# Softmax denominators of two head groups at once on 64 by 32 array tiles, with copied rows and a reordered first batch

## The chip, the cores and the metric

One core of one Trainium2 chip. The metric is the device time of one execution in microseconds (us), the median of several executions. All runs told here are of the state that the records call fast. PE is TensorE, PEld its weight loads, DVE VectorE, ACT ScalarE, POOL GpSimd, SP SyncE. A "q" behind a name (ACTq, SPq) is that engine's queue of transfers.

## The reference

Attention with normalised q and k, followed by a feed-forward block, in float32:

```python
# q, k, v: (batch 8, heads 12, seq 448, head_dim 64)
q_n, k_n = rmsnorm(q, g_q), rmsnorm(k, g_k)
scores = q_n @ k_n.T / 8
attn = exp(scores - max); attn = attn / (sum(attn) + 1e-9)
x = (attn @ v) reshaped to (3584 tokens, 768)
h = x @ w_in                          # w_in: (768, 2048)
g = max(h, 0) + alpha * min(h, 0)
out = g @ w_out                       # w_out: (2048, 768)
```

## The kernel before

Work is cut into 24 groups of four heads, three groups to a batch element. For each group the kernel squares and reduces q and k, takes the inverse root on ScalarE, scales (on GpSimd, early on partly on VectorE), transposes (from group 8 on by a transposing DMA on SyncE's queue), and then makes seven score tiles. ScalarE takes each tile's exponential. TensorE sums them over the keys (dn, the denominators) and multiplies them with v (av). ScalarE inverts dn as exp(-ln(dn)), and VectorE multiplies av with it.

```python
def root(y, nms="qk"):                       # ScalarE, 0.33 + 0.23 us
    ...
    nc.scalar.activation(out=rr, in_=ss, func=AF.Ln, scale=1.0 / D, bias=epsb[:, 0:1])
    nc.scalar.activation(out=rr, in_=rr, func=AF.Exp, scale=-0.5)

def scale(y, nm):
    t = ld.tile([128, J, 2, D], FP16, name="qs", tag="qs", bufs=4)
    eng = nc.vector if (y, nm) in ((0, "k"), (1, "q")) else nc.gpsimd
    eng.tensor_mul(out=..., in0=nat[y, nm], in1=rr_t[y][...])

def score(y, j):                             # two buffers in all
    sc = pss.tile([128, 2, 512], FP32, name="sc", tag="sc")
    ...                                      # four matmuls, 64 by 64 tiles

def over_keys(name, y, weights):             # 28 matmuls, four at once
    acc = psa.tile([128, 2, 512], FP32, name=name, tag="acc")   # one buffer
    e = expT[y]
    for j in range(J):
        for g in range(2):
            for par in range(2):
                nc.tensor.matmul(out=acc[ds(64 * par, 64), g, :S],
                    lhsT=weights(g, par, j), rhs=e[ds(64 * g, 64), j, par, :],
                    start=(j == 0), stop=(j == J - 1))
    return acc

def den(y):
    rden[y] = over_keys("dn", y, lambda g, par, j: ones[ds(64 * g, 64), :])
def log(y):
    r = att.tile([128, 2, S], FP32, name="rden", tag="rden")
    nc.scalar.activation(out=r, in_=rden[y][:, :, :S], func=AF.Ln)
    rden[y] = r
def invert(y):
    nc.scalar.activation(out=rden[y], in_=rden[y], func=AF.Exp, scale=-1.0)
def attv(y):
    av = over_keys("av", y, ...v...)
    nc.vector.tensor_mul(out=xT[b][:, :, i, :], in0=av[:, :, :S], in1=rden[y])
```

The order is written by hand as a list of bursts. Each burst has two or three score tiles, at most one dn or one av, the root of a later group, and some feed-forward units that fill TensorE while ScalarE works: "up" (hT, six matmuls, then ah on ScalarE and gT on VectorE) and "down" (op, 16 matmuls):

```python
for n in range(NB):
    ...
    for t in tiles[:2]:
        score(*t); soft(*t)                  # soft: the exponential
    if n in dens: den(dens[n])
    if n in avs:  attv(avs[n])
    for t in tiles[2:]:
        score(*t); soft(*t)                  # the third tile
    if n in dens: log(dens[n]); invert(...)
    if n in roots: root(y); scale(y, "q"); scale(y, "k"); turn_dma(y)
    ...                                      # feed-forward units
```

## Time and profile before

| | before |
|---|---|
| time, median of three runs | 456.1 us (455.84 to 456.34) |
| span of the profiled run, mean granted clock | 454.8 us, 0.994 |
| TensorE busy, ScalarE busy | 94%, 64% |

The span is cut into 40 equal slices in this part of the page. A digit is the busy share in tenths. PEclk is the granted TensorE clock in tenths of full speed.

```profile
PE   7677889989999999999999999999999999999996
...
PEclk9989999999999999999999999999999999999999
```

TensorE is nearly full from the eighth slice on, at full clock. What little the score matmuls wait is told by their group (busy us, mean ns, then the idle time before them and who ended it):

```profile
L217 PE MATMUL sc<-qT,kT 64*64 64x448 f16 x672 | 53.8, 364 | 8.6 <-ACT expT L229 5.9
```

To see more than the page tells, I also summed the trace's times from each matmul's start to the next one's start, and split each into **work** (at most a matmul's normal pace), **mode switches** (0.09 us where the tiling changes), **waits**, and **half clock** (the excess of matmuls that run close together while the granted clock is halved). This bookkeeping is mine, from the trace's records and not from a view. Counted a second time with other limits for "close together", waits and half clock move against each other by up to some 5 us; the sums stay. For the kernel before it gives 404.4 of work, 11.3 of switches, 31.2 of waits and 1.6 us of half clock, 448.6 in all. The rest of the span lies ahead of the first matmul and behind the last.

### The profile page before, as it was taken

The page shows a single profiled execution, that of the slowest core. Times are in us where ns is not written, and L with a number is a line of the kernel's source. Part 1 is how long each engine was busy: PE and PEld are TensorE (multiplying, and loading weights), DVE is VectorE, ACT ScalarE, POOL GpSimd, SP SyncE. Part 2 cuts the span into 40 slices and gives each one's busy share as a digit, 9 for nine tenths or more (in the row PEclk, how much of TensorE's full clock was granted, in tenths as well). Part 3 has the DMA queues.
Part 4 walks back from the last instruction along what each step waited for, and adds up shares of the span by engine and source line. Part 5 has one row for each costly group of instructions (what it writes and reads, how often), then busy time and mean ns, then how long its engine had stood idle before and what let it go on. Part 6 is the DMA issues. An engine that isn't in the chain of part 4 may idle for free.

```text
span 454.8 us, 9094 instructions
## 1 busy us (share of the span) xinstructions
PE 426.9 (94%) x3843; PEld 229.8 (51%) x3843; DVE 206.0 (45%) x295; ACT 289.9 (64%) x402; POOL 171.9 (38%) x127
## 2 busy tenths in 40 slices
PE   7677889989999999999999999999999999999996
PEld 3333444555445555455545555455555555455563
DVE  3735353735374545355454545345564333343421
ACT  4878897567677757748786758658785847423300
POOL 5888764560560550750571450750541100000000
PEclk9989999999999999999999999999999999999999
DMA  8999994195547633785666633665352410111122
GB/s 190 239 251 235 220 255 101 23 188 124 132 80 165 156 64 94 87 176 148 120 115 141 157 79 80 114 158 139 76 91 46 76 37 1 37 35 36 35 71 69
DMA packets 60169, 52.77 MB, mean 116 GB/s; under 512 B 32720, under 2 KB 56672, under 8 KB 60128
## 3 DMA queue, kind: packets, MB, share of 16 engines
q1 hardware_dynamic: 47584, 39.37, 37.1%
q0 software_dynamic: 11808, 11.81, 16.5%
q10 hardware_dynamic: 736, 1.02, 1.0%
q8 instruction: 30, 0.49, 0.5%
q14 instruction: 11, 0.09, 0.1%
HBM read 45.62 MB, written 11.01 MB: 125 GB/s over the span
## 4 chain that ended last, share of the span: by engine, by line
PE 78%; ACT 12%; DMA 3%; DVE 3%; POOL 1%; issue 1%; SPq 0%; POOLq 0%
PE op L301 31%; PE hT L284 18%; PE hTa L284 9%; PE sc L217 7%; ACT expT L229 6%; PE av L240 5%; PE dn L240 5%; DMA nat<-in_k_dram 3%; ACT ah L292 2%; PE opa L301 2%; DVE gT L293 2%; ACT rden L255 1%; PE tps L193 1%; ACT rden L260 1%; POOL qs L158 1%
## 5 line engine op out<-in xcount | busy, mean ns | idle before, releaser
L229 ACT ACTIVATE expT<-sc,expb 128x896 f16<-128x896 f32 x168 | 157.9, 1007 | 21.2 <-PE sc L217 21.1
L301 PE MATMUL op<-w_out_sb,gT 128*128 128x384 f16 x848 | 145.9, 326 | 2.1 <-DVE gT L293 2.0
L158 POOL TENSOR_TENSOR qs<-nat,rr 128x896 f16<-128x896 f32 x46 | 79.0, 1738 | 178.8 <-issue 158.3
L284 PE MATMUL hT<-xT,w_in_sb 128*128 128x448 f16 x558 | 117.1, 353 | 3.6 <-DVE gT L293 3.5
L301 PEld LDWEIGHTS <-gT 128*128 128x128 f16 x896 | 84.6, 98 | 65.5 <-issue 12.3
L284 PEld LDWEIGHTS <-w_in_sb 128*128 128x128 f16 x768 | 73.7, 98 | 73.7 <-issue 9.6
L292 ACT ACTIVATE ah<-hT,cols 128x448 f16<-128x448 f32 x93 | 59.0, 636 | 59.6 <-PE hT L284 59.5
L293 DVE TENSOR_TENSOR gT<-hT,ah 128x448 f16<-128x448 f32 x93 | 58.0, 624 | 77.8 <-ACT ah L292 77.8
L135 POOL TENSOR_TENSOR sq<-nat 128x896 f32<-128x896 f32 x44 | 73.1, 1682 | 2.5 <-DMA nat<-in_q_dram 2.3
L328 DVE COPY osb<-op 128x384 f32<-128x384 f32 x51 | 28.4, 557 | 85.3 <-PE op L301 85.3
L217 PE MATMUL sc<-qT,kT 64*64 64x448 f16 x672 | 53.8, 364 | 8.6 <-ACT expT L229 5.9
L292 ACT ACTIVATE ah<-hTa,cols 128x448 f16<-128x448 f32 x35 | 22.2, 633 | 49.4 <-PE hTa L284 49.4
L141 DVE TENSOR_REDUCE ss<-sq 128x14 f32<-128x896 f32 x48 | 49.7, 1076 | 6.5 <-ACT sq L133 6.5
L284 PE MATMUL hTa<-xT,w_in_sb 128*128 128x448 f16 x210 | 45.4, 352 | 0.0
L217 PEld LDWEIGHTS <-kT 64*64 64x64 f16 x672 | 19.2, 105 | 38.4 <-issue 28.7
L268 DVE TENSOR_TENSOR xT<-av,rden 128x896 f16<-128x896 f32 x24 | 26.2, 1090 | 26.1 <-PE av L240 26.1
L240 PE MATMUL av<-expT,vt 64*64 64x448 f16 x672 | 36.0, 350 | 1.9 <-ACT rden L255 1.9
L240 PE MATMUL dn<-expT,ones 64*64 64x448 f16 x672 | 36.0, 350 | 0.2 <-DVE gT L293 0.2
L293 DVE TENSOR_TENSOR gT<-hTa,ah 128x448 f16<-128x448 f32 x35 | 21.8, 624 | 31.3 <-ACT ah L292 31.3
L240 PEld LDWEIGHTS <-vt 64*64 64x64 f16 x672 | 20.6, 107 | 13.8 <-issue 3.3
L240 PEld LDWEIGHTS <-ones 64*64 64x64 f16 x672 | 20.6, 108 | 12.1 <-issue 1.1
L255 ACT ACTIVATE rden<-dn 128x896 f32<-128x896 f32 x24 | 22.3, 931 | 2.4 <-PE dn L240 2.4
(39 smaller groups left out, 133.1 us busy)
## 6 DMA issues: line engine op xcount, KB each, us to landing
out_dram<-osb SPq DMA_DIRECT2D x54, 192.0 KB, 2.7
nat<-in_q_dram SPq DMA_DIRECT2D x46, 224.0 KB, 5.9
nat<-in_k_dram SPq DMA_DIRECT2D x46, 224.0 KB, 6.0
vt<-in_v_dram POOLq DMA_DIRECT2D x16, 336.0 KB, 7.4
w_in_sb<-in_moe_w_in_dram POOLq DMA_DIRECT2D x4, 768.0 KB, 15.0
w_out_sb<-in_moe_w_out_dram POOLq DMA_DIRECT2D x4, 768.0 KB, 10.8
nat<-in_q_dram ACTq DMA_DIRECT2D x2, 224.0 KB, 4.6
nat<-in_k_dram ACTq DMA_DIRECT2D x2, 224.0 KB, 5.8
```

Source lines behind the costliest of these rows:

```text
L135: nc.gpsimd.tensor_mul(out=sqf, in0=src, in1=src)
L141: nc.vector.tensor_reduce(out=ss_t[y][:, "qk".index(nm)].rearrange("p h j -> p (h j)").unsqueeze(2), in_=sqs[y, nm], axis=AXIS_X, op=ALU.add,)
L158: eng.tensor_mul(out=t.rearrange("p j h d -> p h j d"), in0=nat[y, nm], in1=rr_t[y][:, "qk".index(nm)].unsqueeze(3).broadcast_to((128, 2, ...
L217: nc.tensor.matmul(out=sc[ds(64 * g, 64), par, :S].rearrange("p (j c) -> p j c", j=J), lhsT=kT[ds(64 * par, 64), j, g, :], rhs=qT[ds(64 * ...
L229: nc.scalar.activation(out=expT[y][:, j], in_=scs[y, j][:, :, :S], func=AF.Exp, scale=QK_SCALE, bias=expb[:, 0:1],)
L240: nc.tensor.matmul(out=acc[ds(64 * par, 64), g, :S], lhsT=weights(g, par, j), rhs=e[ds(64 * g, 64), j, par, :], start=(j == 0), stop=(j == ...
L255: nc.scalar.activation(out=r, in_=rden[y][:, :, :S], func=AF.Ln)
L284: nc.tensor.matmul(out=hT[:, :S], lhsT=w_in_sb[:, c, ts(ft, 128)], rhs=x[:, c, :], start=(c == order[0]), stop=(c == order[-1]),)
L292: nc.scalar.activation(out=ah, in_=hT[:, :S], func=AF.Copy, scale=alpha_sb[:, ft : ft + 1])
L293: nc.vector.tensor_max(out=gT[:, ft, ds((b & 1) * S, S)], in0=hT[:, :S], in1=ah)
L301: nc.tensor.matmul(out=op[:, :OH], lhsT=gT[:, ft, ts(t, 128)], rhs=w_out_sb[:, ft, ds(oh * OH, OH)], start=(ft == 0), stop=(ft == NF - 1),)
L328: nc.vector.tensor_copy(out=o[:, ds(oh * OH, OH)], in_=op[:, :OH])
```

## The change

Its intent: the denominators need only 32 columns of ones per group, so two groups fit side by side on 64 by 32 tiles, eight matmuls at once, and a pair costs TensorE what one group cost. The first two batch elements (groups 0 to 5) stay single. The pair's sums then lie in 32 partitions per group and half, while the product with av wants 64; so ScalarE writes two inverses, and four DMA copies, issued on ScalarE's own queue, fill the other 32 partitions.

```diff
+    PD = min(6, NG)
+    EB = 3
-        sq = ld.tile([128, 2 * J, D], FP32, name="sq", tag="sq", bufs=4)
+        sq = ld.tile([128, 2 * J, D], FP32, name="sq", tag="sq", bufs=3)
-        eng = nc.vector if (y, nm) in ((0, "k"), (1, "q")) else nc.gpsimd
+        eng = nc.vector if (y, nm) in ((0, "k"), (1, "q"), (2, "q"), (3, "q")) else nc.gpsimd
-            expT[y] = att.tile([128, J, 2, S], FP16, name="expT", tag="expT")
+            expT[y] = att.tile([128, J, 2, S], FP16, name="expT", tag="expT", bufs=EB)
+        dn = psa.tile([128, 2, 512], FP32, name="dn2", tag="acc")
+        for j in range(J):
+            for par in range(2):
+                for n, y in enumerate(ys):
+                    for g in range(2):
+                        nc.tensor.matmul(
+                            out=dn[ds(64 * par + 32 * n, 32), g, :S],
+                            lhsT=ones[ds(64 * g, 64), :32],
+                            rhs=expT[y][ds(64 * g, 64), j, par, :], ...)
+    def invert(ys):
+        ...
+        for n, y in reversed(list(enumerate(ys))):
+            nc.scalar.activation(out=rden[y], in_=r, func=AF.Exp, scale=-1.0)
+        if len(ys) == 2:
+            for n, y in enumerate(ys):
+                for c in range(2):
+                    nc.scalar.dma_start(
+                        out=rden[y][ds(64 * c + 32 * (1 - n), 32)],
+                        in_=rden[y][ds(64 * c + 32 * n, 32)],
+                    )
-        ah = ffn.tile([128, S], FP16, name="ah", tag="ah", bufs=3)
+        ah = ffn.tile([128, S], FP16, name="ah", tag="ah", bufs=2)
-    turn_at[2] = av_at[0]
+    turn_at[2] = av_at[0] + 1
+        for y in roots.get(n, ()):           # now ahead of log and invert
+            root(y)
+            ...
         if n in dens and not lead:
             log(dens[n])
-        if n in roots:                       # was behind them
...  # cut: the list of bursts (72 in place of 66), the places of the jobs,
...  # the order of the first batch, the last output piece
```

## The prediction

> **What bounds the kernel now.** I read the page first (busy time, then the chain of waits), then the groups of instructions, then the timeline of a few bursts. A burst here is two or three score tiles, then perhaps a denominator pass (dn) or a product with v (av), then some feed-forward units: "up" (hT, 6 matmuls, 1.13 us) and "down" (op, 16 matmuls, 2.60 us).
>
> ```profile
> PE 426.9 (94%) x3843; PEld 229.8 (51%) x3843; DVE 206.0 (45%) x295; ACT 289.9 (64%) x402; POOL 171.9 (38%) x127
> ...
> PE 78%; ACT 12%; DMA 3%; DVE 3%; POOL 1%; issue 1%; SPq 0%; POOLq 0%
> ...
> L229 ACT ACTIVATE expT<-sc,expb 128x896 f16<-128x896 f32 x168 | 157.9, 1007 | 21.2 <-PE sc L217 21.1
> ...
> L240 PE MATMUL dn<-expT,ones 64*64 64x448 f16 x672 | 36.0, 350 | 0.2 <-DVE gT L293 0.2
> ...
> L255 ACT ACTIVATE rden<-dn 128x896 f32<-128x896 f32 x24 | 22.3, 931 | 2.4 <-PE dn L240 2.4
> ```
>
> TensorE holds 78% of the chain that ended last and hardly waits: dn had 0.2 us of idle time before it in the whole run. ScalarE is next at 64%. Until about 92 us the chain is mixed (ScalarE's exponentials, DMA, GpSimd); from there to the end it is almost only TensorE. So TensorE time saved after 92 us counts, as long as ScalarE keeps up within each burst. How close that is, a burst shows (start us, length us, engine, what):
>
> ```profile
> 150.42 0.57 PE L217 MATMUL sc<-qT,kT 64*64 64x448 f16 x8
> ...
> 150.83 1.49 PE L240 MATMUL dn<-expT,ones 64*64 64x448 f16 x28
> 151.06 2.80 ACT L229 ACTIVATE expT<-sc,expb 128x896 f16<-128x896 f32 x3
> ...
> 153.73 0.93 ACT L255 ACTIVATE rden<-dn 128x896 f32<-128x896 f32 x1
> 154.70 0.95 ACT L260 ACTIVATE rden<-rden 128x896 f32<-128x896 f32 x1
> ...
> 157.42 0.57 PE L217 MATMUL sc<-qT,kT 64*64 64x448 f16 x8
> ...
> 159.14 0.36 PE L217 MATMUL sc<-qT,kT 64*64 64x448 f16 x4
> ```
>
> Counted from its first score, this burst has exponentials until 3.44 us, the logarithm until 4.24, the inverse until 5.23. The next burst begins at 7.00, and its third score tile is reached at 8.72. That third tile matters: there are two score buffers, so it needs the first exponential of its own burst. Where ScalarE is late, TensorE stops exactly there, with everything behind it. The burst at 88 us, which has no feed-forward units to hide behind, shows it:
>
> ```profile
> 93.22 2.79 ACT L229 ACTIVATE expT<-sc,expb 128x896 f16<-128x896 f32 x3
> ...
> 94.26 0.38 PE L217 MATMUL sc<-qT,kT 64*64 64x448 f16 x4 [0.36 <-ACT expT L229]
> ```
>
> **What the Trainium skill says.** "TensorEngine Tiling (Array Packing)", section Tiling Modes: 64 by 32 gives eight tiles that work at once, 64 by 64 four, and a change of the mode drains the engine. The trace agrees for four: the chain has dn's 28 matmuls in 1.32 us, seven rounds of 0.189 us, with 0.189 us also the time of one matmul of 448 columns (six hT in 1.13). A change between 64 by 64 and the whole array costs 0.09 us (third score at 152.15, next op at 152.44, less 0.19). Eight at once is shown by no run yet. "Perfetto Trace Analysis", section Per-engine timelines, DMA Instruction — HWDGE: the sequencer that issues a transfer is free for its next instruction only at the end of the reported window; the data move outside it. The trace agrees: ScalarE's table load starts when its queue has finished issuing, 0.64 us each.
>
> ```profile
> 1.51 0.64 ACTq L101 DMA_DIRECT2D nat<-in_k_dram  x1
> ...
> 2.18 1.28 ACT L450 ACT_TABLE_LOAD   x1 [2.18 <-issue]
> ```
>
> "TensorE: Matmul & The Clock Gate", section The HAM clock gate: an idle window of about 3.4 us halves the clock. Here the clock was 0.61 between 30 and 34 us, after TensorE had done little from 26.9 on.
>
> **The change, part by part.**
>
> Removed: groups 6 to 23 become nine pairs. A pair has 56 matmuls, as two groups had, but if eight run at once it takes seven rounds, 1.32 us in place of 2.65. Nine times 1.32 is 11.9 us of TensorE. ScalarE saves one logarithm of 0.93 us a pair.
>
> Added on TensorE: dn now stands in another mode between second and third score, two changes of 0.09 us in eight pairs (the ninth has no scores): 1.5 us. The schedule has 72 bursts, it had 66; each is two changes: 6 x 0.19 = 1.1 us. Net 9.3 us saved.
>
> Added on ScalarE: in one burst it now does both inverses, and issues four transfers behind them. Those have to wait for its own inverses, so the sequencer stands still until then, and then spends some 0.55 us on each issue (nearly all issues from 48 to 224 KB took 0.47 to 0.67 us, whatever their size): 2.2 us. In seven of nine pairs the burst also has the root of a later group (0.33 + 0.23 us). One pair then looks like this, for a burst with one down and one up, all from rows above: exponentials until 3.44, root 4.0, logarithm 4.8, inverses 6.8, issues 9.0, ah of the up unit 9.7, first exponential of the next burst 10.6. TensorE's burst is 7.00 less one up (1.13) plus two changes: 6.06; its third score is reached 1.72 later, at 7.8. It waits 2.8 us. With one down alone both sides are earlier (6.65 and 9.7): 3.0 us. With two up units and no root (first pair): ah lies between logarithm and inverses, ScalarE comes at 10.7, TensorE at 6.3: 4.4 us.
>
> There is a second hold. The built program's waits show that each transfer on ScalarE's queue reuses one of eight semaphores, and waits for the transfer that used it before. In three pairs (8 and 9, 12 and 13, 16 and 17) the fourth copy's predecessor is the transpose of k of the group whose root stands in the same burst: root at 4.0, two GpSimd products of 1.74 us until 7.5, transpose landed 3.3 us later (median) at 10.8. ScalarE is then free at 11.3 rather than 9.0: 2.3 us more.
>
> Sum of the waits: 4.4 + 5.3 + 2.8 + 5.1 + 3.0 + 5.1 + 3.0 + 3.0, and none for the last pair, which has no scores after it: 31.7 us.
>
> The landing itself, about 2 us as for small stores, falls beside the next burst and holds only the product with av on VectorE: small.
>
> Start and end: the scaling of q for groups 2 and 3 goes from GpSimd to VectorE, beside that of k. In the chain such a scaling is a piece of 1.7 us; twice that is 3.4, I take 3 us. The last output copy is one piece in place of two on two engines: 0.5 us less.
>
> All waits as worked out: 456.1 - 9.3 - 3.5 + 31.7 = 475. No waits at all: 443. **I choose 466**, about seven tenths of the waits. They rest on a timetable that assumes nothing else shifts, and a schedule so carefully made may have been tried where they are smaller; but the third score waiting for the first exponential is in the trace already.
>
> **Rivals.** (1) *TensorE's saving goes through* and ScalarE absorbs the rest, as its 64% suggest. For it: over the five bursts of a pair ScalarE has about 23 us of work against TensorE's 30. Against: an average doesn't help, two buffers let TensorE run ahead by one tile. It gives about 443 to 447. (2) *Issues are cheap* (0.1 us for 32 rows) and no semaphore holds: each wait shrinks by 1.8 us and the three holds go, the sum becomes about 11 us: 454. Against: I found no issue under 0.47 us in the trace. (3) *Eight tiles do not run at once*, for want of instructions or read ports: TensorE saves nothing, plus 2.6 us of mode changes; waits then shrink by 1.3 us a pair: around 475 again. (4) *The longer waits throttle the clock*: four of 4.4 to 5.3 us, each followed by up to 3 us at half speed: up to 6 us on top, 481. (5) *Transfers are late* and av's product holds the one accumulator: some 1 to 2 us a pair more; against it, DMA is at a half after 100 us and small stores land in 2 to 2.7 us.
>
> **Range and chances.** No waits and a good start is the low end, 447 with a little margin given away; all waits with a throttled clock the high end, 482. Faster by over 2% needs under 447, so nearly no waits: 0.14. Within 2% is 447 to 465: half of the waits or cheap issues: 0.36. Slower: 0.50.
>
> **What would show it.** Right: 504 dn matmuls in nine stretches of 1.32 us; issues on ScalarE's queue of about 0.55 us, 36 of them; behind them idle time of ScalarE put down to issue; third scores waiting 2 to 5 us for expT, some 30 us in all where before had 5.9. Wrong: stretches of dn near 2.6 us (eight tiles), issues near 0.1 us, or third scores that don't wait. The prediction fails upward if the clock drops after those waits, downward if ScalarE's work in the pair's burst overlaps in a way that the timetable doesn't have.

## The result

| | before | after |
|---|---|---|
| time, median | 456.22 us (455.84 to 458.04, 4 runs) | 513.26 us (510.84 to 514.56, 4 runs) |
| span and mean clock, profiled run | 454.8 us, 0.994 | 509.1 us, 0.939 |

The changed kernel is slower: ratio 1.1235, 95% interval 1.1182 to 1.1289. A ratio is the mean time of one kernel's fast runs over that of the other's of the same rounds, so it is not quite the ratio of the medians quoted.

The page of the changed kernel, busy share and slices:

```profile
PE 438.9 (86%) x3837; PEld 224.1 (44%) x3837; DVE 207.8 (41%) x297; ACT 284.0 (56%) x392; POOL 169.0 (33%) x125
...
PE   7866798898697798799499699599697799999996
...
PEclk9887999898799799999699899889898999999999
```

Where TensorE stood at 9 throughout, dents come again and again from the eleventh slice on, and in the slices beside them the clock is down. TensorE's *busy* time even rose, from 426.9 to 438.9 us, though it has fewer rounds to do: matmuls at half speed are longer. The groups of instructions, scores and dn, and then the waits (in all, how often, longest):

```profile
L219 PE MATMUL sc<-qT,kT 64*64 64x448 f16 x672 | 56.2, 383 | 49.6 <-ACT expT L231 43.4
...
L263 PE MATMUL dn<-expT,ones 64*32 64x448 f16 x504 | 15.0, 375 | 0.0
```

```profile
PE sc L219 <- ACT expT L231: 43.4, 20, 6.8
```

The scores' wait for an exponential grew from 5.9 to 43.4 us. The timeline of the second pair (start us, length us; an issue's row covers all of its count, with the time between them) shows how it comes about. The view begins at 156 us and ends at 171.5, and counts only what it holds: the pair's dn has 56 matmuls, and the last row's op has 16.

```profile
155.64 1.49 PE L263 MATMUL dn<-expT,ones 64*32 64x448 f16 x49
...
159.09 0.92 ACT L275 ACTIVATE rden<-dn 128x896 f32<-128x896 f32 x1
...
160.04 1.93 ACT L283 ACTIVATE rden<-rden 128x896 f32<-128x896 f32 x2
...
162.01 5.64 ACTq L288 DMA_DIRECT2D rden<-rden  x4
...
162.41 1.23 SPq L170 DMA_TRANSPOSE kT<-qs  x1
...
167.69 2.80 ACT L231 ACTIVATE expT<-sc,expb 128x896 f16<-128x896 f32 x3 [5.72 <-DMA rden<-rden]
...
168.75 0.59 PE L219 MATMUL sc<-qT,kT 64*64 64x448 f16 x4 [6.77 <-ACT expT L231]
...
169.27 2.74 PE L332 MATMUL op<-w_out_sb,gT 128*128 128x384 f16 x8
```

The inverses end at 161.97. Then ScalarE issues four copies, and is free again only at 167.65: by the records of the single issues three took until 163.9, and the fourth began at 167.13. It waits for the semaphore of the transpose of k of a later group, which landed at 167.11. The next burst's exponentials stand behind them, so the third score starts at 168.75, after 6.77 us of an idle TensorE. The op behind it takes 2.74 us for eight matmuls; 16 took 2.60 before. The three stretches of this pair, as a table by stretch (us, then busy time and count of PE, PEld, DVE, ACT and POOL, then the clock, the DMA share and GB/s):

```profile
155.00:162.00 7.00, 6.99 (x122) 3.53 (x121) 1.34 (x3) 6.16 (x8) 4.63 (x3) 1.00 0.84 196
162.00:169.00 7.00, 0.25 (x4) 0.13 (x3) 1.09 (x1) 1.30 (x2) 2.02 (x2) 0.83 1.01 228
169.00:175.00 6.00, 6.00 (x26) 2.78 (x22) 0.86 (x2) 1.50 (x2) 0.00 (x0) 0.63 0.42 105
```

Full work, then nearly nothing, then full busy time at a clock of 0.63: that is the price of one pair. My bookkeeping, in us:

| | work | switches | waits | half clock | sum |
|---|---|---|---|---|---|
| before | 404.4 | 11.3 | 31.2 | 1.6 | 448.6 |
| after | 391.9 | 13.8 | 75.8 | 21.8 | 503.3 |
| difference | -12.5 | +2.5 | +44.6 | +20.2 | +54.7 |

The eight pairs that have scores after them waited 4.3, 6.8, 3.3, 6.4, 3.9, 6.0, 3.9 and 3.3 us, 38.0 in all. In the second, fourth and sixth, the three longest, the fourth issue was held as it is here.

### The profile page after: what moved, and what is told of

Same layout as the page of the kernel before. It is cut to its first block, busy times and chain, and to the rows that moved or that the text cites. A ratio compares the mean times of both kernels' runs of the same rounds, so it can differ in the third digit from the quotient of the medians.

```text
span 509.1 us, 9140 instructions
## 1 busy us (share of the span) xinstructions
PE 438.9 (86%) x3837; PEld 224.1 (44%) x3837; DVE 207.8 (41%) x297; ACT 284.0 (56%) x392; POOL 169.0 (33%) x125
## 5 line engine op out<-in xcount | busy, mean ns | idle before, releaser
L332 PE MATMUL op<-w_out_sb,gT 128*128 128x384 f16 x848 | 154.3, 338 | 0.0
L315 PE MATMUL hT<-xT,w_in_sb 128*128 128x448 f16 x576 | 126.1, 363 | 6.9 <-DVE gT L324 6.9
L332 PEld LDWEIGHTS <-gT 128*128 128x128 f16 x896 | 87.1, 101 | 70.0 <-issue 19.6
L160 POOL TENSOR_TENSOR qs<-nat,rr 128x896 f16<-128x896 f32 x44 | 75.4, 1732 | 115.1 <-issue 49.6
L137 POOL TENSOR_TENSOR sq<-nat 128x896 f32<-128x896 f32 x44 | 73.9, 1686 | 119.2 <-DVE ss L143 110.5
L324 DVE TENSOR_TENSOR gT<-hT,ah 128x448 f16<-128x448 f32 x96 | 59.9, 624 | 104.2 <-ACT ah L323 103.9
L219 PE MATMUL sc<-qT,kT 64*64 64x448 f16 x672 | 56.2, 383 | 49.6 <-ACT expT L231 43.4
L315 PE MATMUL hTa<-xT,w_in_sb 128*128 128x448 f16 x192 | 41.5, 352 | 0.0
L242 PE MATMUL av<-expT,vt 64*64 64x448 f16 x672 | 36.8, 355 | 3.8 <-ACT rden L275 3.1
L242 PEld LDWEIGHTS <-vt 64*64 64x64 f16 x672 | 20.7, 108 | 16.2 <-issue 5.5
L283 ACT ACTIVATE rden<-rden 128x896 f32<-128x896 f32 x24 | 22.9, 953 | 0.7
L275 ACT ACTIVATE rden<-dn 128x896 f32<-128x896 f32 x15 | 13.6, 909 | 4.6 <-PE dn L242 3.6
L263 PE MATMUL dn<-expT,ones 64*32 64x448 f16 x504 | 15.0, 375 | 0.0
```

Source lines behind the costliest of these rows:

```text
L137: nc.gpsimd.tensor_mul(out=sqf, in0=src, in1=src)
L160: eng.tensor_mul(out=t.rearrange("p j h d -> p h j d"), in0=nat[y, nm], in1=rr_t[y][:, "qk".index(nm)].unsqueeze(3).broadcast_to((128, 2, ...
L219: nc.tensor.matmul(out=sc[ds(64 * g, 64), par, :S].rearrange("p (j c) -> p j c", j=J), lhsT=kT[ds(64 * par, 64), j, g, :], rhs=qT[ds(64 * ...
L242: nc.tensor.matmul(out=acc[ds(64 * par, 64), g, :S], lhsT=weights(g, par, j), rhs=e[ds(64 * g, 64), j, par, :], start=(j == 0), stop=(j == ...
L283: nc.scalar.activation(out=rden[y], in_=r, func=AF.Exp, scale=-1.0)
L315: nc.tensor.matmul(out=hT[:, :S], lhsT=w_in_sb[:, c, ts(ft, 128)], rhs=x[:, c, :], start=(c == order[0]), stop=(c == order[-1]),)
```

## The experiments

Theory A: ScalarE's issues, and the holds in them, delay the next burst's first exponential, the third score waits for it, and the halved clock follows from those waits. Rivals: the new schedule as a whole (buffers, places of the jobs), the start, dn in the new mode, the landing of the copies. The 18 kernels ran each beside runs of the kernel before on the same chip (456.2 to 457.5 us).

| run | median us | ratio to before (95%) | waits | half clock |
|---|---|---|---|---|
| changed kernel | 513.26 | 1.1235 (1.1182 to 1.1289) | 75.8 | 21.8 |
| no_copies (wrong result) | 464.75 | 1.0168 (1.0118 to 1.0218) | 42.1 | 8.1 |
| copies_sp | 485.38 | 1.0630 (1.0588 to 1.0673) | 60.5 | 12.6 |
| no_pairs | 482.53 | 1.0572 (1.0541 to 1.0603) | 50.1 | 11.4 |
| dn_twice | 525.03 | 1.1536 (1.1471 to 1.1601) | 80.2 | 18.5 |
| root_late | 498.84 | 1.0923 (1.0877 to 1.0969) | 67.9 | 19.1 |
| keep_warm | 506.42 | 1.1086 (1.1036 to 1.1136) | 51.7 | 15.5 |
| root3_scale | 509.58 | 1.1132 (1.1076 to 1.1187) | 73.5 | 22.9 |
| no_pairs_old_bufs | 464.78 | 1.0189 (1.0155 to 1.0222) | 40.1 | 4.9 |
| scale_pool | 511.93 | 1.1196 (1.1134 to 1.1258) | 75.2 | 25.6 |
| root_late_sp | 477.19 | 1.0465 (1.0398 to 1.0533) | 58.4 | 5.4 |
| late_sp_start | 473.56 | 1.0359 (1.0322 to 1.0395) | 54.7 | 4.6 |
| late_sp_start_two | 469.12 | 1.0270 (1.0230 to 1.0311) | 48.1 | 5.8 |
| unpaired_start | 460.51 | 1.0071 (1.0025 to 1.0117) | 36.3 | 1.5 |
| unpaired_start_late | 464.89 | 1.0173 (1.0134 to 1.0213) | 38.8 | 3.1 |
| bare_start_late (wrong result) | 468.90 | 1.0254 (1.0201 to 1.0307) | 50.9 | 4.3 |
| bare_start (wrong result) | 458.05 | 1.0017 (0.9968 to 1.0066) | 40.7 | 2.8 |
| turn_sp_start | 475.83 | 1.0409 (1.0354 to 1.0463) | 56.3 | 4.4 |
| turn_sp_start_two | 471.52 | 1.0306 (1.0251 to 1.0362) | 53.0 | 6.0 |

All but the three marked ones give the right result.

### The copies left out

```diff
-        if len(ys) == 2:
-            for n, y in enumerate(ys): ... nc.scalar.dma_start(...)
```

> The four copies of a pair are left out, so half of the inverse rows are wrong and the output is wrong on purpose; everything else is as in the changed kernel. Theory A (the copies hold ScalarE's queue, and the third score of the next burst waits for it): the eight long waits of av to sc for expT shrink from 39 us to about 7 us (0.6 to 0.9 us each, 2.2 us for the first pair), the clock is hardly throttled (half-speed time from 20 us to under 5), time about 460 to 468 us. Rival B (the pair itself, that is both inverses in one burst, or the schedule of 72 bursts, makes the waits): waits stay over 20 us, time over 490 us.

The result is wrong (half of the inverses are missing; relative error 0.96). The time is 464.75 us, as theory A had it: the four copies are worth 48.5 of the 57.0 us that the change lost. The timeline of the second pair without them:

```profile
155.34 1.93 ACT L283 ACTIVATE rden<-rden 128x896 f32<-128x896 f32 x2
...
157.18 2.79 ACT L231 ACTIVATE expT<-sc,expb 128x896 f16<-128x896 f32 x3
...
158.22 0.38 PE L219 MATMUL sc<-qT,kT 64*64 64x448 f16 x4 [0.71 <-ACT expT L231]
```

The next burst's exponentials follow the inverses at once, and the third score waits 0.71 us in place of 6.77. In the list of waits the scores' wait for expT is 9.4 us in place of 43.4:

```profile
PE sc L219 <- ACT expT L231: 9.4, 15, 1.5
```

The half clock goes along with the waits, from 21.8 to 8.1 us (under 5 was expected), though nothing about the clock was touched.

### The copies on SyncE's queue

```diff
-                    nc.scalar.dma_start(
+                    nc.sync.dma_start(
```

> The same four copies, issued from SyncE's queue in place of ScalarE's; result right. Theory A: ScalarE is as free as without copies, so about the time of no_copies, plus a few us where the copies stand behind transposes in SyncE's queue and VectorE's product waits for them: 462 to 475 us. Rival C (the copies' landing, not their place in ScalarE's queue, is what holds TensorE): no better than the changed kernel, 505 us or more.

485.38 us, so my expectation of 462 to 475 was a miss. ScalarE is as free as without copies (the same pair's third score waits 0.70 us), but in SyncE's queue the copies stand behind the transposes of the later group, which wait for GpSimd's scaling:

```profile
156.42 1.93 ACT L283 ACTIVATE rden<-rden 128x896 f32<-128x896 f32 x2
...
160.35 2.48 SPq L288 DMA_DIRECT2D rden<-rden  x4
...
163.36 1.09 DVE L299 TENSOR_TENSOR xT<-av,rden 128x896 f16<-128x896 f32 x1 [6.00 <-DMA rden<-rden]
164.51 0.54 PE L315 MATMUL hT<-xT,w_in_sb 128*128 128x448 f16 x2 [1.36 <-DVE xT L299]
```

The inverses end at 158.35, the copies are issued from 160.35 on, and VectorE's product waits 6.00 us for them, and hT for the product. The cost of a copy depends on what stands in front of it in its queue: moved, the wait became another one, on VectorE.

### The root behind the inverses again

```diff
+        if n in dens and not lead: log(dens[n]); invert(...)
         for y in roots.get(n, ()): root(y); scale(...); turn_dma(y)
-        if n in dens and not lead: log(dens[n]); invert(...)
```

> The root of a later group, with its scalings and transposes, stands after the inverses and copies in the program, as in the kernel before; copies still on ScalarE's queue. Theory A with its second hold (the fourth copy of three pairs waits for the transpose of k started in the same burst): the three waits of 6.0 to 6.9 us fall to 3.3 to 4 us, as the others; the sum of third-score waits goes from 39 to about 30 us, the half-speed time from 20 to about 14 us: 496 to 502 us. Rival F (the hold by the semaphore is not what lengthens these three): all waits as they were, 510 us or more. If the later roots make transposes late, new waits for kT show.

498.84 us, within what was expected. With the transposes now issued after the copies, no copy waits for one. The four issues of the second pair take 2.45 us, not 5.64:

```profile
158.46 2.45 ACTq L288 DMA_DIRECT2D rden<-rden  x4
...
162.48 0.38 PE L219 MATMUL sc<-qT,kT 64*64 64x448 f16 x4 [3.35 <-ACT expT L231]
```

The waits of the eight pairs are 4.3, 3.4, 2.8, 2.8, 3.4, 2.8, 3.4 and 4.0 us, and the three held pairs are no longer apart. Their sum is 26.7 us in place of 38.0. So the hold, with the root's 0.56 us that no longer stand in the chain, is about 11 us of these waits. Most of the rest is the issues themselves: without copies the same waits come to under 5 us.

### dn twice

```diff
+        for again in range(2):
             for j in range(J): ...   # the 56 matmuls of dn2
```

> The denominators of each pair are computed twice over (the second pass starts the sums anew, so the result is right): 1.32 us more TensorE work in each pair, 11.9 us in all. Theory A: in eight pairs TensorE waits 3 to 7 us soon after, so the added work lies inside that wait: time within 3 us of the changed kernel, the waits about 1.3 us shorter each. Rival E (TensorE's own work still sets the time): 12 us more, about 525 us.

525.03 us: 11.8 more, where my theory said that the third score waits anyway and hides it (within 3 us). It fell. dn stands ahead of the third score, its exponential stands ahead of the logarithm on ScalarE, and so the whole chain of ScalarE moves along:

```profile
240.26 2.84 PE L264 MATMUL dn<-expT,ones 64*32 64x448 f16 x112
...
243.04 0.38 PE L219 MATMUL sc<-qT,kT 64*64 64x448 f16 x4
...
243.47 1.01 ACT L231 ACTIVATE expT<-sc,expb 128x896 f16<-128x896 f32 x1 [1.17 <-PE sc L219]
```

ScalarE idles 1.17 us for it. In reverse this says that the shorter dn of the pairs did save what it should; and the 2.84 us for 112 matmuls, half of it for 56, show once more that eight ran at once.

### Filling the wait with matmuls

```diff
+        if n in avs and n - 1 in dens and len(dens[n - 1]) == 2 and tiles[2:]:
+            spin(17)
         for t in tiles[2:]: score(*t); soft(*t)
```

> Seventeen dummy matmuls (3.2 us) before the third score of the burst after each pair, so that TensorE is busy while it waits; nothing else changed, result right. Theory G (after the waits TensorE's clock is halved for 3 to 7 us, and this costs about 12 us in dense matmuls and 20 us in all): half-speed stretches after the pairs vanish, time 493 to 502 us. Rival H (the slow stretches come from elsewhere, or the third score is simply reached later): 510 us or more.

506.42 us, short of the 493 to 502 that I expected. 17 idle matmuls last 3.39 us. Pairs with short waits keep the clock (half clock 21.8 to 15.5 us), but in the held pairs 3.7 to 4.2 us of idle time remain behind the spins, and the clock halves all the same:

```profile
248.85 0.59 PE L219 MATMUL sc<-qT,kT 64*64 64x448 f16 x4 [3.73 <-ACT expT L231]
...
249.37 5.30 PE L332 MATMUL op<-w_out_sb,gT 128*128 128x384 f16 x16
```

16 op matmuls in 5.30 us, twice their 2.60. The half clock is a consequence of the idle time and not a load of its own; it can be bought off in part, and that gains 7 us, not 20.

### The start: root3_scale and scale_pool

```diff
-    turn_at[2] = av_at[0] + 1          # root of group 3 in burst 8
+    turn_at[2] = av_at[0]              # burst 7, as before   (root3_scale only)
-        ... in ((0, "k"), (1, "q"), (2, "q"), (3, "q")) else nc.gpsimd
+        ... in ((0, "k"), (1, "q")) else nc.gpsimd            # (both)
```

> Of the first batch's reordering only two things are undone: the turn of group 2 and with it the root of group 3 stand one burst earlier again, and q of groups 2 and 3 is scaled on GpSimd again. Theory I (these two make the third product with v 3.7 us late): that product is back within 1 us of the kernel before, the half-speed stretch at 40 to 47 us is gone; time 4 to 6 us below the changed kernel, 507 to 510 us. Rival J (other parts of the new start, such as the later weight loads, make it late): less than 2 us gained.

> Only the scaling of q of groups 2 and 3 goes back from VectorE to GpSimd; the root of group 3 stays in burst 8. Theory (the two engines, started side by side on the two scalings, hold each other up: 1.09 us on VectorE while GpSimd's grows from 1.69 to 2.59 or the other way round): the split saves under 1.5 us, so giving it back costs nothing much at the start: the third av starts within 1.5 us of the changed kernel's, and the end within 509 to 516. Rival (the split is worth the 3 us that the prediction gave it): the third av starts 3 us or so later than in the changed kernel, and the time is 515 to 518.

The product of the third group with v starts at 45.07 us before, 48.77 after, 47.82 with scale_pool and 43.38 with root3_scale. So the split of the scaling over two engines gained nothing (scale_pool gives it up and is 0.9 us earlier there, 511.93 us in total), and the later root cost over 4 us there. Both totals are within what was expected. Scaling side by side is in the timeline of the changed kernel:

```profile
38.34 2.59 POOL L160 TENSOR_TENSOR qs<-nat,rr 128x896 f16<-128x896 f32 x1 [4.78 <-ACT rr L155]
...
38.30 1.09 DVE L160 TENSOR_TENSOR qs<-nat,rr 128x896 f16<-128x896 f32 x1 [0.49 <-ACT rr L155]
```

Before, GpSimd did both in 3.34 us:

```profile
36.09 3.34 POOL L158 TENSOR_TENSOR qs<-nat,rr 128x896 f16<-128x896 f32 x2 [3.67 <-ACT rr L153]
```

GpSimd's product alone takes 1.69 us. Started 0.04 us after VectorE's, it takes 2.59: 0.90 longer, which is most of VectorE's 1.09. The Trainium skill says this: "SBUF — State Buffer", section "SBUF: two separate sides", has VectorE with two inputs from SBUF and GpSimd share a pair of ports as an exclusive lock, where the later one waits for the whole instruction of the first. The trace agrees. I hadn't looked there when I took the two for parallel. Split, they save 3.34 less 2.63 us, 0.7 us, and not half.

root3_scale reaches the third product 5.4 us earlier than the changed kernel, but ends only 3.7 us earlier. From 60 us on its clock was halved for 58 us in place of 48: all eight waits are followed by half clock there and not six, although they are no longer (36.8 us in place of 38.0). So it seems to depend on how the waits fall, and small differences between kernels with such waits say little.

### No pairs

```diff
-    PD = min(6, NG)
+    PD = NG                                       # no_pairs
-    EB = 3      ... "sq" bufs=3 ... "ah" bufs=2
+    EB = 2      ... "sq" bufs=4 ... "ah" bufs=3   # no_pairs_old_bufs, in addition
```

> Denominators one group at a time throughout (no 64 by 32 tiles, no copies), all the rest of the change kept: reordered first batch, three expT buffers, other places for roots and reductions. Theory A: the loss is the pairs'; what stays is the 4 to 5 us that the changed kernel is behind at the fourth product with v: 458 to 463 us. Rival D (the reordering is a large part of the loss): 470 us or more.

> As no_pairs (482.5 us), with the buffers of the kernel before: two for expT, four for sq, three for ah; the schedule of bursts is the same. Theory K (with three sq buffers GpSimd's queue stops at a square until VectorE has reduced an earlier one, the scalings behind it and the transposes of k come late, two waits of 5.6 us): those waits are gone, 460 to 466 us. Rival L (the new places of roots and reductions are the cause, whatever the buffers): 476 us or more.

no_pairs was a miss: 482.53 us, not 458 to 463, with neither pairs nor copies (and so with 66 bursts again). The waits name GpSimd, which can't take a fourth buffer for the squares until VectorE has reduced an old one, and then scales and transposes too late:

```profile
POOL sq L137 <- DVE ss L143: 107.8, 17, 11.5
...
PE sc L219 <- DVE kT L181: 12.2, 4, 5.5
```

With the old buffer counts that wait is 13.8 us and the time 464.78, within the 460 to 466 expected. Three buffer counts went back together; that the squares' is the one that counts is read from the waits (those for kT fall from 12.2 to 1.7 us) and was not tried alone. So the third expT buffer, which pairs need, is paid with buffers elsewhere. In the paired schedule the squares' wait is there too (110.5 us in the changed kernel, 76.2 in no_copies), but no_copies shows that it costs little there (kT waits of 2.8 us only).

### Copies on SyncE with the right order

Can a correct kernel reach what no_copies promises? root_late_sp has the copies on SyncE and the root behind the inverses, so that the copies are ahead of the transposes in the queue. late_sp_start adds the start as before; late_sp_start_two has only two score tiles in a pair's dn burst:

```diff
-        wide = n in dens and dens[n][0] >= G or n in avs and avs[n] >= G
+        wide = n in dens and G <= dens[n][0] < PD or n in avs and avs[n] >= G
```

> The copies go to SyncE's queue, and the root of the later group with its scalings and transposes is written after the pair's logarithm, inverses and copies, so that the copies stand ahead of the transposes in SyncE's queue. Theory (the cost on ScalarE is the issues and their hold; on SyncE with the transposes in front the copies came 2 us late): the third scores wait no more than in the run without copies (0.9 to 1.7 us a pair), VectorE's product waits under 1 us for a copied inverse, half clock 6 to 9 us: 463 to 471 us, against 485 for the copies on SyncE alone and 499 for the late root alone. Rival (root first is what feeds VectorE and GpSimd; delayed, the transposed k comes too late, a new wait of some us per group): 475 to 485, with waits of VectorE for kT that grow above 9 us.

> As the kernel with late root and copies on SyncE, and the first batch's root of group 3 one burst earlier with the scaling of q on GpSimd again, as before. Theory: the start's 5.5 us come back where the clock is not already lost to the later waits: 4 to 6 us under the kernel without the early root, 457 to 467 us. Rival (the clock window takes it back, as it did in the run of this change alone: 3.7 of 5.5 us): within 2 us of the kernel without it.

> As the last, with two score tiles in a pair's denominator burst in place of three, so that no third score stands behind dn there: 76 bursts in place of 72. Theory (what is left is ScalarE's own work in the pair's burst, two inverses in place of one): the waits behind dn go to the first score of the next burst, which ScalarE reaches about 1 us before TensorE; the burst count costs 0.8 us; 452 to 464 us, so as fast as the kernel before within 2%. Rival (ScalarE's work is only moved; with more bursts the exponentials come one burst later and ScalarE is short elsewhere): equal to or up to 8 us above the last.

477.19, 473.56 and 469.12 us: all three above their ranges, though each step goes the way that was expected. The third scores wait 1.5 us at most and the clock is nearly whole (0.986), so theory A's part is cured. The early start is worth 3.6 us here (its third product is 3.3 us earlier, and so is its end), where the clock doesn't interfere. What remains is the rival of the first text: waits for a late kT grew from 2.5 to 15.3 us (15.4 with the early start). With two tiles they are 5.8 us; what holds that kernel back I did not take apart.

### What the schedule could give at best

Still open was why the kernels without copies or without pairs are 8 us behind the kernel before. Four runs: no pairs and old buffers with the old start (unpaired_start), the same with the late root (unpaired_start_late), and pairs without copies with the old start, with the late root (bare_start_late) and with the early root (bare_start).

> As the kernel without pairs and with the old buffers (464.8 us, 8 us above the kernel before), with the first batch's start as before: group 3's root one burst earlier, its and group 2's scaling of q on GpSimd. Theory (5 us of those 8 are the start, the prediction had -3 there): third av back to about -1.7 us against the kernel before, total 459 to 462. Rival (the start is made up by later waits and the 8 us come from the order and places of the later groups' roots and jobs): 463 to 466.

> As the last, with the root written behind the logarithm and the inverse again, as in the kernel before. Theory (root first delays each logarithm by 0.56 us, which the third score of the next burst sees in some bursts): third scores' waits for the exponential near the 5.9 us of before, total 456 to 460, level with the kernel before. Rival (root first was put there because GpSimd's products and the transposes need it in the new places of the jobs): kT waits grow, 460 to 464.

> Wrong on purpose: the pairs stay, all four copies are left out, root behind the inverses, start as before. What pairing could give at best in this schedule. Theory (the copies, the start and the root's place are all that stands against TensorE's 10 us): 450 to 456 us, under the kernel before. Rival (pairing itself, three groups' expT in flight with 72 bursts, two inverses in one burst and only three buffers for the squares, costs what it saves): 458 to 465.

> Wrong on purpose: pairs without the four copies, root ahead of the logarithm as in the changed kernel, first batch's start as before. The floor of pairing in this schedule. Theory (of the 8 us that the kernel without copies loses, 4 to 5 are the start; a late root costs 4 to 8 through a later kT): 458 to 462. Rival (half clock takes the start back): 463 to 466.

unpaired_start and bare_start came out as the theories had it; the two with the late root came out above even their rivals' ranges. The start is worth 4.3 us without pairs (464.78 to 460.51) and 6.7 us with them (464.75 to 458.05; the runs of a pair of numbers are of different lots). The late root costs 4.4 us without pairs and 10.9 us with them. So the changed kernel's order, root first, was right for the new places of the jobs; moving it back cures the hold and makes kT late.

bare_start is the answer to what pairing could give here: 458.05 us, ratio 1.0017, level with the kernel before, *with the copies free*. Its work is 11.5 us below that of the kernel before and its switches 2.6 above, and its waits are 9.5 us above (40.7, before 31.2): by the list of waits, scores for exponentials 10.1 us in place of 5.9, for a kT of the later groups 2.8 in place of none, hT for gT 6.9 in place of 3.5. That ScalarE's second inverse in one burst is behind these waits is likely, but I did not take it out by itself.

### Root first, copies ahead of the transposes

```diff
         for y in roots.get(n, ()): root(y); scale(y, "q"); scale(y, "k")
-            if y >= TD: turn_dma(y)
         if n in dens and not lead: log(dens[n]); invert(...)   # copies on SyncE
+        for y in roots.get(n, ()):
+            if y >= TD: turn_dma(y)
```

> Correct results. Root and scalings stay ahead of the logarithm; only the issue of the transposes is written behind the copies, and the copies go to SyncE's queue, so that neither the root nor the copies are late. Start as before. Theory (the two costs of moving the copies to SyncE were the order in its queue and the late root): within 1 to 6 us of the floor, 460 to 467. Rival (transposes behind four issues of 0.6 us are late again, and kT waits as with the late root): 468 to 474.

> The last with two score tiles in a pair's denominator burst. Two tiles took 4.4 us off with the late root. Theory: the same here, 456 to 463, about level with the kernel before. Rival (those 4.4 us were waits that the late root had made): 460 to 468, no better than the last.

475.83 and 471.52 us: both above even their rivals' ranges (468 to 474, 460 to 468). Two tiles gained 4.3 us, as expected, but from a level that was too high. SyncE's queue is the reason again:

```profile
187.10 2.51 SPq L288 DMA_DIRECT2D rden<-rden  x4
...
189.71 2.70 SPq L170 DMA_TRANSPOSE qT<-qs  x1
192.51 1.24 SPq L170 DMA_TRANSPOSE kT<-qs  x1
...
196.00 0.38 PE L219 MATMUL sc<-qT,kT 64*64 64x448 f16 x4 [2.92 <-DVE kT L181]
```

Four issues take 2.51 us, and the first transpose behind them 2.70 us where it takes 1.25 alone in the changed kernel. It follows copies that are still in flight; whether it waits for them, this row doesn't tell. The transposed k comes late, and a score waits 2.92 us for it; kT waits are 17.2 us in all. So nothing beat the kernel before: the best correct variant with pairs has 469.12 us, and the best correct one of all, 460.51, has none.

What stays open: whether the copies can be had for less on another path (VectorE writing 64 rows, or a matmul that spreads them) was not tried.

## Why the prediction was right or wrong

**TensorE's saving: right.** Predicted were -11.9 for the pairs, +1.5 and +1.1 for mode changes, -9.3 in all; measured are -12.5 and +2.5, -10.0. Eight tiles do run at once: 15.0 us busy for nine pairs. Rival 3 is out.

**The mechanism of the waits: right; its size, and the discount on it: wrong.** The wait stands where it was placed, at the third score behind the pair's burst, released by expT. The three pairs with a hold were named beforehand and are the three longest: 6.8, 6.4 and 6.0 us against 5.3, 5.1 and 5.1 predicted; the other five 18.8 us against 16.2. The uncut sum was 31.7, the runs show 38.0. Two terms were short. An issue on ScalarE took 0.51 to 0.9 us, some 2.5 to 3 us for four, not 2.2. And the transpose of k was taken to land 3.3 us after its issue began, the median of the kernel before; in the three pairs with a hold it took 4.7, 4.9 and 4.5 us. Then comes a step that failed outright: "I choose 466, about seven tenths of the waits". Nothing in a view spoke for that discount. It took about 9 us off a sum of 475 that was itself too low, and the reason given, that a careful schedule may have been tried where waits are smaller, was a guess about the author and not a reading.

**The clock: left among the rivals, and mis-sized; the largest part of the miss.** The sum has nothing for it, and the rival "up to 6 us" for four waits; measured are 20.2 us more. Six of the eight waits were followed by half clock (the two of 3.3 us were not), not four, and each costs up to 3 us. Not all of it is theirs: no_copies, without such waits, has 8.1 us of half clock too. The changed kernel's clock is halved at 13, 40, 98 and 122 us as well, ahead of all of these waits, where the kernel before has one stretch, at 30 us; and at 389 us, after a wait of 2.9 us for gT. The Trainium skill has the pattern in "TensorE: Matmul & The Clock Gate", section "HAM oscillation — how this bites in real kernels": a wait that crosses the window throttles the array again, each time. The trace agrees for six of the eight waits, with a clock of 0.63 after the second pair's. Once I expected waits of about 3 us and more in eight places, the term belonged in the sum.

**The start: wrong in sign.** Predicted -3.5; the third group's product started 3.7 us later than before, and undoing the two parts gives 3.6 to 6.7 us, depending on the run. The root one burst later was in the diff and not in my sum, and the scaling on two engines is not parallel.

**The sum.** With the measured terms: 456 - 10 + 38 + 20, and about 7 for other waits, the start among them, is 511, the time of the profiled run; the median is 513. This divides up one trace and is no further test. Of the 47 us between 466 and 513 the clock is 20; the third scores' waits are 15 (9 the discount, 6 the short terms); the start and other waits are 10, about 7 in place of -3.5; the rest is the profiled run's distance from the median. So the step that failed is the sum's choice of terms: nothing for the clock, seven tenths of the waits, and a gain at the start. The likeliest direction, slower at 0.50, was right; the range's upper end, all waits with a throttled clock, was 482, since it took the predicted waits, the 6 us for the clock, and no loss at the start.

**What I said would show it.** 504 dn matmuls in nine short stretches, 36 issues on ScalarE's queue, third scores that wait 2 to 5 us (3.3 to 6.8), some 30 us in all (43.4 with the usual 5.9), and a clock that drops as the case in which the prediction fails upward: all seen. Rival 2 is out, as no issue of a copy took under 0.51 us. Of rival 5 half came true: the copies landed 3.7 us after their issue in the median, not about 2, and VectorE's product waited 17.4 us for them in all, but no matmul of the changed kernel waited for that product. One reading after the result was wrong, too: that dn's time lies inside the wait (dn_twice).

**Readings of the trace before.** Three are looser than they sound, and none of them moved the sum. The two issues ahead of the table load took 0.73 and 0.64 us, not 0.64 each; 130 of the 156 plain issues on the two queues lie between 0.47 and 0.67 us, and the longest took 1.42; and TensorE was busy for 2.14 of the 4 us from 26 to 30, so the half clock from 30 on does not show that a whole idle window came before it.

## What to carry to other kernels

A queue of transfers on a computing engine is part of that engine's chain: count its issues one by one, and ask what each has to wait for in order, its own source, the one in front, and the transfer whose semaphore it reuses. A sum of waits worked out from rows is not to be cut for luck; and where it puts TensorE to rest again and again, the halved clock belongs in it (here it followed all six waits of 3.9 us and more). Before a saving on the busiest engine is bought with work on the next one, run the version where that work is left out: if this floor (458.05 us here) is level with the kernel before, placing that work elsewhere in the same schedule has nothing left to win.

## What the Trainium skill lacked or had wrong

- "TensorEngine Tiling (Array Packing)", section Tiling Modes, says that a mode change drains the array, without a figure. Here a change between 64 by 64 or 64 by 32 and the whole array costs 0.09 us, and one between 64 by 64 and 64 by 32 as much. That 64 by 32 gives eight tiles at once was right: 56 matmuls of 448 columns in about 1.45 us.
- "DMA: Bandwidth & Descriptors", section Rules for kernel authors, says that spreading transfers over engines only saves sequencer issue time. It has no figure for how long an issue holds ScalarE when its queue is used. Here it was 0.51 to 0.9 us on ScalarE, some 2.5 to 3 us for four small copies, and the copies cost the kernel 48.5 us in all.
- No page tells that an issue may be held because the built program reuses a semaphore, until another engine's transfer with that semaphore has landed. Here that held ScalarE until 167.13 us in one pair, and gave the three longest waits, 6.0 to 6.8 us.
- "TensorE: Matmul & The Clock Gate", section The HAM clock gate, has the clock halved after at least one idle window of about 3.4 us. Shorter waits were enough here: one of 2.9 us in the changed kernel (at 388 us) and one of 2.8 us in root_late (at 198 us) were followed by half clock. Two of 3.3 us in the changed kernel kept the clock, as did one of 3.4 us in root_late (at 274 us). So the length of a wait alone does not tell.
